# First weights' factors kept by units in DRAM, first keys in two halves, last block transposed on TensorE

## The chip, the cores and the metric

The kernel runs on one core of one Trainium2 chip. The metric is the device time of one execution in microseconds; a number is the median of several executions. A profile is one execution more, taken with the hardware profiler, and is a little longer than an unprofiled one. Engines are named as the profile does: PE is TensorE's matmul and PEld its weight load, DVE is VectorE, ACT is ScalarE, POOL is GpSimd, SP is SyncE, which only issues transfers here.

## The reference

Two blocks in a row. The first is attention with a hash: every query and key gets a bucket of 6 sign bits, and a query attends only to keys in its own bucket. The second is a layer with a squared ReLU. Cut to what matters:

```python
# q, k, v: (4, 8, 768, 64); proj: (64, 6); w_in: (512, 2048); w_out: (2048, 512)
q_bucket = bits(q @ proj > 0)                # 6 bits to one number
k_bucket = bits(k @ proj > 0)
scores = q @ k.T / 8
scores = where(q_bucket == k_bucket, scores, -1e9)
attn = softmax(scores)
x = (attn @ v) laid out as (3072, 512)       # tokens by heads
h = x @ w_in
g = maximum(h, 0) ** 2
out = g @ w_out                              # (3072, 512)
```

The weights arrive as 64-bit floats, and the kernel rounds them to 32 bits itself.

## The kernel before

Attention goes by 16 pairs of heads. For each pair PE hashes q and k with `projs`, ACT makes the bits, PE makes the scores (the bits' product keeps other buckets away), ACT takes the exponential, PE multiplies with v. Beside it DVE rounds the weights, piece by piece.

The layer is computed by a scheme of seven products in place of eight. Each matrix is cut in four blocks, and sums of blocks are the factors. For `w_in` these factors are made during attention and kept in DRAM as `w_in_7`, seven of them, and read back by units of 128 columns of the hidden layer, eight units for each of three chunks of 1024 tokens. For `w_out` the scheme is applied twice, with 49 factors in `w_out_49`, which are made beside the first chunk's hidden layer and written by POOL's queue.

```python
w_in_7 = p_d.tile([P, 7, NFT // 2, HF], FP32, name="w_in_7")     # 128, 7, 2, 1024, in DRAM

def keep_weight(i):
    ...                                      # once for each half of the columns
    for dst, f, h in (
        (w_in_7[:, 0], 0, 0), (w_in_7[:, 1], nf, 0), (w_in_7[:, 2], nf, 1), (w_in_21, 0, 1)
    ):
        nc.sync.dma_start(out=dst[:, :, at], in_=ins[j][:, f:f + nf, h])

def sums_in(c):                              # four times, 256 columns each
    ...
    for n in range(4):
        nc.sync.dma_start(out=w_in_7[:, 3 + n, :, c * NS:(c + 1) * NS], in_=sums[n])

def load_unit(n, pool=p_i):                  # two buffers, and one more at the start
    if n < NCHUNK * NR and n not in w_unit:
        r = n % NR
        w_unit[n] = pool.tile([P, 7, NFT // 2, P], FP32, name="w_unit", ...)
        nc.sync.dma_start(
            out=w_unit[n].rearrange("p l f c -> p (l f) c"),
            in_=w_in_7.rearrange("p l f c -> p (l f) c")[:, :, r * P:(r + 1) * P],
        )
```

The start. `load_first` brings q and k of the first pair, one head on SP's queue and one on ACT's; `keep_busy` gives PE matmuls on a constant so that it is not idle; `turn` hands out one of three PSUM buffers.

```python
def constants():
    nc.gpsimd.memset(projs, 0.0)
    for h in range(2):
        nc.gpsimd.dma_start(out=projs[h * D:(h + 1) * D, 0:N], in_=proj)
    ...

def first_keys():                            # the bits of the first pair's keys, on DVE
    bits[0, 1] = t = all_bits[0][1]
    for c in range(2):
        ...
        for h in range(2):
            nc.vector.tensor_scalar(out=t[...], in0=hashed[0, 1][at, h, 0:HS], ..., op0=ALU.is_gt)
        nc.vector.tensor_scalar(out=t[:, cut], in0=t[:, cut], scalar1=spans, scalar2=bases, ...)

load_first()
nc.vector.memset(busy, 1.0)
keep_busy(8)
...
first_features(0, 0)                         # PE transposes q, ACT copies
first_features(0, 1)
keep_busy(2, 256)
first_features(1, 0)                         # PE transposes k, DVE copies
hash_bits(0, turn("hash"), (0,))
first_features(1, 1)
banks = turn("hash")
for c in range(2):
    hash_bits(0, banks, (1,), (c,))
keep_busy(4)
signs(0, 0)                                  # ACT: the bits of q
first_keys()
for pr in range(NP):
    ...
    score(pr, 0)
    score(pr, 1)
    ...
```

The end. A block of the output is finished transposed: DVE turns it in squares of 32 into one of two buffers `ot`, and four transfers put the squares in their places.

```python
def put_out(i, ih, jh, n, o, lo=0):
    w = o.shape[1]
    ot = p_y.tile([P, HN], FP32, name="ot", bufs=2)[:, 0:w]
    nc.vector.transpose(out=ot, in_=o)
    ...
    for a in range(P // 32):
        queue = nc.gpsimd if (ih, jh) == (1, 1) else nc.sync
        if (i, ih, jh) == (NCHUNK - 1, 1, 0) and a % 2:
            queue = nc.scalar
        queue.dma_start(out=out[at, ...], in_=ot[a * 32:(a + 1) * 32]...)

def close(ih, jh, n):
    o = outs[ih, jh, n // 2]
    o[1] += 1
    if (i, ih, jh, n // 2) == (NCHUNK - 1, 1, 0, 1):      # the last block: by halves
        lo = n % 2 * QN
        put_out(i, ih, jh, n // 2, o[0][:, lo:lo + QN], lo)
    elif o[1] == 2:
        put_out(i, ih, jh, n // 2, o[0])
```

A second function, `general`, computes everything in the plain way when a guard finds inputs too large for the fast one. It does not run here, but it reads `w_in_7` too.

Of the kernel before, what the change touches and what calls it, by code (L numbers as in the profile page):

```python
# [8 lines left out]
FP32 = mybir.dt.float32  # L9
# [6 lines left out]
ALU = mybir.AluOpType  # L16
# [18 lines left out]
def kernel(  # L35
# [24 lines left out]
    PIECE = 512  # L60
# [19 lines left out]


    HF, HD, NR, NQ = DFF // 2, DM // 2, NFF // 2, NFF // 4
    w_in_7 = p_d.tile([P, 7, NFT // 2, HF], FP32, name="w_in_7")
    w_in_21 = p_d.tile([P, NFT // 2, HF], FP32, name="w_in_21")
    w_out_1 = p_d.tile([P, NFF, DM], FP32, name="w_out_1")
    w_out_49 = p_d.tile([7, P, 7, NQ, P], FP32, name="w_out_49")
# [15 lines left out]
    def turn(name):  # L102

        return ps_s.tile([P, 2, 512], FP32, name=name, tag="turn")
# [78 lines left out]
    def keep_weight(i):  # L183

        t = goals.pop(i)
        j, c = divmod(i, NIN)
        if j >= 2:
            nc.sync.dma_start(out=w_out_1[:, i - 2 * NIN], in_=t)
        elif c == NIN - 1:
            at = slice(j * PIECE, (j + 1) * PIECE)  # L190
            nf = NFT // 2
            for dst, f, h in (
                (w_in_7[:, 0], 0, 0), (w_in_7[:, 1], nf, 0), (w_in_7[:, 2], nf, 1), (w_in_21, 0, 1)
            ):
                nc.sync.dma_start(out=dst[:, :, at], in_=ins[j][:, f:f + nf, h])

# [21 lines left out]

    def constants():
        N = NBITS
        nc.gpsimd.memset(projs, 0.0)
        for h in range(2):
            nc.gpsimd.dma_start(out=projs[h * D:(h + 1) * D, 0:N], in_=proj)
        for t in (gains, lifts, spans, bases):
            nc.vector.memset(t, 0.0)
        nc.vector.memset(excess, -896.0)
        for h in range(2):
            r = h * D  # L230
            nc.vector.memset(gains[r:r + N + 1], -FAR / 2 * N)
# [28 lines left out]
    def load_first():  # L260

        for src, name in ((q, "q_nat"), (k, "k_nat")):
            t = p_qk.tile([P, SB, 2, D], FP32, name=name)
            for h, queue in enumerate((nc.sync, nc.scalar)):
                queue.dma_start(
                    out=t[:, :, h], in_=src[0, h].rearrange("(t p) d -> p t d", t=SB)
                )
            nat[0, name] = t

# [58 lines left out]
    def hash_bits(pr, banks, ws=(0, 1), cs=(0, 1)):  # L328


        for w in ws:
            hashed[pr, w] = banks
            for c in cs:
                g = 2 * w + c
                for h in range(2):
                    rows = slice(h * D, (h + 1) * D)
                    nc.tensor.matmul(  # L337
                        out=banks[g * NR_B:(g + 1) * NR_B, h, 0:HS], lhsT=projs[rows],
                        rhs=feat[pr, w][rows, c * HS:(c + 1) * HS], start=True, stop=True,
                    )  # L340

    def signs(pr, w):
        bits[pr, w] = t = all_bits[pr % 2][w]
        for c in range(2):
            at = slice((2 * w + c) * NR_B, (2 * w + c + 1) * NR_B)
            for h in range(2):
                nc.scalar.activation(  # L347
                    out=t[h * D:h * D + NR_B, c * HS:(c + 1) * HS], in_=hashed[pr, w][at, h, 0:HS],
                    func=ACTF.Sign, scale=HUGE, bias=lifts[at],
                )  # L350

    def first_keys():

        bits[0, 1] = t = all_bits[0][1]
        for c in range(2):
            at = slice((2 + c) * NR_B, (3 + c) * NR_B)
            cut = slice(c * HS, (c + 1) * HS)
            for h in range(2):
                nc.vector.tensor_scalar(
                    out=t[h * D:h * D + NR_B, cut], in0=hashed[0, 1][at, h, 0:HS],  # L360
                    scalar1=0.0, scalar2=None, op0=ALU.is_gt,
                )
            nc.vector.tensor_scalar(
                out=t[:, cut], in0=t[:, cut], scalar1=spans, scalar2=bases, op0=ALU.mult,
                op1=ALU.add,
            )

    def weigh(pr):

# [126 lines left out]
    def sums_in(c):  # L496

        j, h = divmod(c, 2)
        t, at = ins[j], slice(h * NS, (h + 1) * NS)
        nf = NFT // 2  # L500
        sums = [p_t.tile([P, nf, NS], FP32, name=f"s_in{n}", bufs=2) for n in range(4)]
        sums_a(
            t[:, 0:nf, 0, at], t[:, nf:NFT, 0, at], t[:, 0:nf, 1, at], t[:, nf:NFT, 1, at], *sums
        )
        for n in range(4):
            nc.sync.dma_start(out=w_in_7[:, 3 + n, :, c * NS:(c + 1) * NS], in_=sums[n])

# [17 lines left out]
    def load_unit(n, pool=p_i):  # L525

        if n < NCHUNK * NR and n not in w_unit:
            r = n % NR
            w_unit[n] = pool.tile([P, 7, NFT // 2, P], FP32, name="w_unit", bufs=2 if pool is p_i else 1)
            nc.sync.dma_start(  # L530
                out=w_unit[n].rearrange("p l f c -> p (l f) c"),
                in_=w_in_7.rearrange("p l f c -> p (l f) c")[:, :, r * P:(r + 1) * P],
            )

    def sums_x(i, n):

# [18 lines left out]
        spread(pr)  # L555

    with tc.manual_schedule():
        load_first()
        nc.vector.memset(busy, 1.0)
        keep_busy(8)  # L560
        make_identity(nc, ident)
        constants()
# [6 lines left out]
        keep_busy(2, 256)  # L569
        first_features(1, 0)  # L570
        hash_bits(0, turn("hash"), (0,))
        first_features(1, 1)
        banks = turn("hash")
        for c in range(2):
            hash_bits(0, banks, (1,), (c,))
        keep_busy(4)
        signs(0, 0)
        first_keys()

        for pr in range(NP):
# [243 lines left out]
            add_to(t, one, two)  # L826
            return t

        def put_out(i, ih, jh, n, o, lo=0):


            w = o.shape[1]
            ot = p_y.tile([P, HN], FP32, name="ot", bufs=2)[:, 0:w]
            nc.vector.transpose(out=ot, in_=o)  # L834
            m0 = ih * HD + n * P
            at = slice(i * NCH + jh * HN + lo, i * NCH + jh * HN + lo + w)
            for a in range(P // 32):
                queue = nc.gpsimd if (ih, jh) == (1, 1) else nc.sync
                if (i, ih, jh) == (NCHUNK - 1, 1, 0) and a % 2:
                    queue = nc.scalar  # L840
                queue.dma_start(
                    out=out[at, m0 + a * 32:m0 + (a + 1) * 32].rearrange("(c i) j -> i c j", i=32),
                    in_=ot[a * 32:(a + 1) * 32].rearrange("i (c j) -> i c j", j=32),
                )

        def project(i):

# [182 lines left out]
def general(tc, slow, ident, w_in_7, w_in_21, w_out_1, q, k, v, proj, out_v):  # L1030
# [19 lines left out]
    with ExitStack() as stack:  # L1050
# [4 lines left out]
        with tc.If(flag > 0), ExitStack() as inner:  # L1055
# [4 lines left out]
            for src, f, c in (  # L1060
                (w_in_7[:, 0], 0, 0), (w_in_7[:, 1], nf, 0), (w_in_7[:, 2], nf, hf), (w_in_21, 0, hf)
            ):
                nc.sync.dma_start(out=w_in[:, f:f + nf, c:c + hf], in_=src)
# [161 lines left out]
```

## Time and profile before

The median of three executions is 899.83 us (899.75 to 900.01). The profiled execution took 905.62 us, of which the span of the instructions is 903.8 us.

| stage of the span | us | what fills it |
|---|---|---|
| start, up to the first scores | 0 to 12.1 | loads, transposes, hash of the first pair |
| attention, 16 pairs | 12.1 to 337.7 | PE |
| first chunk's hidden layer | 337.7 to 441 | PE, with many transfers beside it |
| the rest of the layer | 441 to 892.6 | PE |
| end | 892.6 to 903.8 | last sums, transposes and transfers |

| transfer | number | KB each | median us to landing |
|---|---|---|---|
| `w_unit` from `w_in_7` (SP) | 24 | 896 | 5.5 |
| `w_in_7` from `in` (SP), `w_in_21` with it | 8 | 512 | 4.0 |
| `w_in_7` from the sums (SP) | 16 | 256 | 2.9 |
| `w_out_49` from sums and factors (POOL) | 28 | 448 | 7.0 and 7.3 |
| weights as they arrive (SP) | 32 | 512 | 5.4 and 4.1 |

How to read the profile's lines: in a timeline a line has its start, its length, the engine, the line of the kernel, the operation, the tile written and the tile read, sizes, the number of instructions merged into it, and in brackets how long the engine was idle just before and what ended that. A line of the stage table has the stretch, its length, each engine's busy time with its number of instructions, the clock granted to PE (1.00 is full), the busy share of the 16 DMA engines (rough, it can pass 1), and GB/s.

### The profile page before, as it was taken

The page shows a single profiled execution, that of the slowest core. Times are in us where ns is not written, and L with a number is a line of the kernel's source. Part 1 is how long each engine was busy: PE and PEld are TensorE (multiplying, and loading weights), DVE is VectorE, ACT ScalarE, POOL GpSimd, SP SyncE. Part 2 cuts the span into 40 slices and gives each one's busy share as a digit, 9 for nine tenths or more (in the row PEclk, how much of TensorE's full clock was granted, in tenths as well). Part 3 has the DMA queues.
Part 4 walks back from the last instruction along what each step waited for, and adds up shares of the span by engine and source line. Part 5 has one row for each costly group of instructions (what it writes and reads, how often), then busy time and mean ns, then how long its engine had stood idle before and what let it go on. Part 6 is the DMA issues. An engine that isn't in the chain of part 4 may idle for free.

```text
span 903.8 us, 11749 instructions
## 1 busy us (share of the span) xinstructions
PE 880.1 (97%) x4292; PEld 503.7 (56%) x4292; DVE 711.4 (79%) x991; ACT 376.0 (42%) x608; POOL 91.7 (10%) x149
## 2 busy tenths in 40 slices
PE   8999999999999999998999999999999999999995
PEld 4444444444444444443688854445888544458884
DVE  5899999999999977796777775668778666777874
ACT  5988788888888842221211112222111122221110
POOL 2000000000000002542000111112000111100002
PEclk9999999999999999998999999999999999999998
DMA  9578679899966318998765734557757455545475
GB/s 185 112 154 135 198 191 183 186 267 243 235 142 164 117 65 259 289 266 250 244 201 154 192 66 133 151 152 237 264 162 171 74 152 151 146 134 156 148 186 85
DMA packets 253407, 158.14 MB, mean 175 GB/s; under 512 B 166496, under 2 KB 215648, under 8 KB 253344
## 3 DMA queue, kind: packets, MB, share of 16 engines
q1 hardware_dynamic: 218448, 84.04, 40.3%
q10 hardware_dynamic: 24160, 37.89, 14.3%
q0 software_dynamic: 10736, 35.40, 12.7%
q8 instruction: 36, 0.59, 0.3%
q14 instruction: 27, 0.22, 0.1%
HBM read 119.28 MB, written 38.01 MB: 174 GB/s over the span
## 4 chain that ended last, share of the span: by engine, by line
PE 88%; DMA 5%; DVE 4%; ACT 1%; issue 1%; ACTq 0%; SPq 0%; DVEq 0%
PE acc L679 54%; PE st L385 17%; PE xo L414 14%; DMA w_unit<-w_in 3%; PE tot L433 2%; PE hash L337 2%; DMA out_dram<-ot 1%; DVE total L404 1%; DMA k_nat<-in_k_dram 1%; ACT bits L347 1%; DVE peaks L720 0%; DVE ot L834 0%; DVE b L769 0%; ACTq L809 0%; ACT e L389 0%
## 5 line engine op out<-in xcount | busy, mean ns | idle before, releaser
L679 PE MATMUL acc<-x,w_unit 128*128 128x512 f32 x384 | 172.2, 600 | 4.2 <-DMA w_unit<-w_in 4.2
L389 ACT ACTIVATE e<-st 128x1024 f32<-128x1024 f32 x192 | 145.2, 810 | 50.1 <-PE st L385 45.6
L385 PE MATMUL st<-feat,feat 64*128 64x512 f32 (+1 forms) x768 | 150.4, 483 | 0.0
L414 PE MATMUL xo<-e,v_nat 128*64 128x512 f32 (+1 forms) x768 | 134.8, 492 | 0.0
L679 PE MATMUL acc<-b,leaf 128*128 128x256 f32 x600 | 132.9, 379 | 0.0
L679 PE MATMUL acc<-t_x,w_unit 128*128 128x512 f32 x288 | 127.8, 593 | 0.5 <-ACT one L686 0.5
L679 PEld LDWEIGHTS acc<-x,w_unit 128*128 128x128 f32 x384 | 73.8, 193 | 96.8 <-issue 90.6
L679 PEld LDWEIGHTS acc<-b,leaf 128*128 128x128 f32 x600 | 114.0, 190 | 16.8 <-issue 1.4
L404 DVE TENSOR_TENSOR total<-total,e 128x1536 f32<-128x1536 f32 x58 | 101.9, 1757 | 3.8
L414 PEld LDWEIGHTS xo<-e,v_nat 128*64 128x64 f32 x768 | 51.3, 136 | 82.4 <-issue 75.0
L679 PEld LDWEIGHTS acc<-t_x,w_unit 128*128 128x128 f32 x288 | 54.5, 190 | 70.2 <-issue 67.7
L768 DVE TENSOR_TENSOR h<-acc,two 128x512 f32<-128x512 f32 x24 | 16.6, 691 | 89.8 <-PE acc L679 89.8
L385 PEld LDWEIGHTS st<-feat,feat 64*128 64x128 f32 x768 | 66.1, 188 | 33.9 <-issue 25.2
L679 PE MATMUL acc<-t,leaf 128*128 128x256 f32 x336 | 76.6, 380 | 0.7 <-ACT one L686 0.4
L686 ACT COPY two<-acc 128x512 f32<-128x512 f32 (+1 forms) x45 | 21.9, 486 | 132.6 <-PE acc L679 120.3
L347 ACT ACTIVATE bits<-hash,lifts 32x384 bf16<-32x384 f32 x124 | 71.0, 573 | 4.9 <-PE hash L337 1.6
L686 ACT COPY one<-acc 128x512 f32<-128x512 f32 (+1 forms) x45 | 21.9, 486 | 122.4 <-PE acc L679 76.7
L679 PEld LDWEIGHTS acc<-t,leaf 128*128 128x128 f32 x336 | 63.6, 190 | 10.5 <-DVE t L492 1.1
L769 DVE SCALAR_TENSOR_TENSOR b<-h 128x512 f32<-128x512 f32 x96 | 64.3, 690 | 2.5
L385 PE MATMUL st<-bits,bits 64*128 64x256 bf16 (+1 forms) x384 | 63.2, 325 | 2.4 <-ACT e L389 1.2
L679 PE MATMUL acc<-b_t,leaf 128*128 128x256 f32 x240 | 54.2, 380 | 2.0 <-issue 2.0
L679 PEld LDWEIGHTS acc<-b_t,leaf 128*128 128x128 f32 x240 | 45.4, 190 | 8.8 <-issue 2.7
(124 smaller groups left out, 867.1 us busy)
## 6 DMA issues: line engine op xcount, KB each, us to landing
leaf<-w_out ACTq DMA_DIRECT2D x142, 256.0 KB, 3.0
w_unit<-w_in SPq DMA_DIRECT2D x24, 896.0 KB, 5.5
raw<-in_moe_w_in_dram SPq DMA_DIRECT2D x16, 512.0 KB, 5.4
raw<-in_moe_w_out_dram SPq DMA_DIRECT2D x16, 512.0 KB, 4.1
w_out<-sums POOLq DMA_DIRECT2D x16, 448.0 KB, 7.0
v_nat<-in_v_dram SPq DMA_DIRECT2D x16, 384.0 KB, 4.3
x_all<-x_t SPq DMA_DIRECT2D x16, 384.0 KB, 3.1
x<-x_all POOLq DMA_DIRECT2D x3, 2048.0 KB, 12.0
```

The lines of the kernel that those rows point to most:

```text
L337: nc.tensor.matmul(out=banks[g * NR_B:(g + 1) * NR_B, h, 0:HS], lhsT=projs[rows], rhs=feat[pr, w][rows, c * HS:(c + 1) * HS], start=True, ...
L347: nc.scalar.activation(out=t[h * D:h * D + NR_B, c * HS:(c + 1) * HS], in_=hashed[pr, w][at, h, 0:HS], func=ACTF.Sign, scale=HUGE, bias=li ...
L385: nc.tensor.matmul(out=st[:, h, 0:hi - lo], lhsT=src[pr, 1][rows, key], rhs=src[pr, 0][rows, lo:hi], start=first, stop=not first,)
L389: nc.scalar.activation(out=e[:, :, lo:hi], in_=st[:, :, 0:hi - lo], func=ACTF.Exp, scale=scale)
L404: nc.vector.tensor_tensor(out=totals[pr], in0=totals[pr], in1=weights[pr, kt][:, :, 0:S], op=ALU.add)
L414: nc.tensor.matmul(out=xo[h * D:(h + 1) * D, lo:hi], lhsT=nat[pr, "v_nat"][:, h, kt * D:(kt + 1) * D], rhs=weights[pr, kt][:, h, lo:hi], s ...
L433: nc.tensor.matmul(out=tot[g * 32:(g + 1) * 32, 0:HS], lhsT=ones, rhs=src[:, h, c * HS:(c + 1) * HS], start=src is srcs[0], stop=src is sr ...
L679: nc.tensor.matmul(out=acc[to], lhsT=a(i), rhs=b(i), start=first and i == 0, stop=last and i == n - 1, skip_group_check=True,)
L686: nc.scalar.copy(out=t, in_=acc[of])
L768: nc.vector.tensor_tensor(out=h, in0=one, in1=two, op=ALU.add)
L769: nc.vector.scalar_tensor_tensor(out=out[:, r], in0=h, scalar=0.0, in1=h, op0=ALU.max, op1=ALU.mult)
```

## The change

Three parts. First, the factors in DRAM are laid out by unit, so that what `load_unit` reads is one stretch per partition; the writes are cut accordingly, and `general` reads them in the new order. Second, the bits of the first pair's keys are made in two halves, the second after the first scores; with it the projection comes by one transfer on ACT's queue in place of two on POOL's, and the memsets of `busy` and `projs` go first on DVE. Third, the last output block is transposed on PE, copied by ACT and DVE, and written by one transfer for each half; half of the transfers of the block before it move from ACT's queue to POOL's.

```diff
-    w_in_7 = p_d.tile([P, 7, NFT // 2, HF], FP32, name="w_in_7")
+    w_in_7 = p_d.tile([NR, P, 7, NFT // 2, P], FP32, name="w_in_7")
 ...
-            for dst, f, h in (
-                (w_in_7[:, 0], 0, 0), (w_in_7[:, 1], nf, 0), (w_in_7[:, 2], nf, 1), (w_in_21, 0, 1)
-            ):
-                nc.sync.dma_start(out=dst[:, :, at], in_=ins[j][:, f:f + nf, h])
+            for n, f, h in (0, 0, 0), (1, nf, 0), (2, nf, 1):
+                put_factor(n, j * PIECE, ins[j][:, f:f + nf, h])
+            nc.sync.dma_start(
+                out=w_in_21[:, :, j * PIECE:(j + 1) * PIECE], in_=ins[j][:, 0:nf, 1]
+            )
+
+    def put_factor(n, c, t):
+        for f in range(NFT // 2):
+            rs = t[:, f].rearrange("p (r c) -> p r c", c=P)
+            nc.sync.dma_start(
+                out=w_in_7[c // P:c // P + rs.shape[1], :, n, f].rearrange("r p c -> p r c"), in_=rs
+            )
 ...
         for n in range(4):
-            nc.sync.dma_start(out=w_in_7[:, 3 + n, :, c * NS:(c + 1) * NS], in_=sums[n])
+            put_factor(3 + n, c * NS, sums[n])
 ...
-            nc.sync.dma_start(
-                out=w_unit[n].rearrange("p l f c -> p (l f) c"),
-                in_=w_in_7.rearrange("p l f c -> p (l f) c")[:, :, r * P:(r + 1) * P],
-            )
+            nc.sync.dma_start(out=w_unit[n], in_=w_in_7[r])
```

```diff
     def constants():
-        nc.gpsimd.memset(projs, 0.0)
-        for h in range(2):
-            nc.gpsimd.dma_start(out=projs[h * D:(h + 1) * D, 0:N], in_=proj)
 ...
     def load_first():                        # in its loop over q and k
+            if src is q:
+                nc.scalar.dma_start(
+                    out=projs[:, 0:NBITS],
+                    in_=proj.rearrange("(o d) n -> o d n", o=1).to_broadcast([2, D, NBITS]),
+                )
 ...
-    def first_keys():
+    def first_keys(c, banks):                # hash, compare and scale one half
+        hash_bits(0, banks, (1,), (c,))
 ...
+        nc.vector.memset(busy, 1.0)
+        nc.vector.memset(projs, 0.0)
         load_first()
-        nc.vector.memset(busy, 1.0)
 ...
         hash_bits(0, turn("hash"), (0,))
+        signs(0, 0)
+        first_keys(0, turn("hash"))
         first_features(1, 1)
-        banks = turn("hash")
-        for c in range(2):
-            hash_bits(0, banks, (1,), (c,))
         keep_busy(4)
-        signs(0, 0)
-        first_keys()
 ...
             score(pr, 0)
+            if pr == 0:
+                first_keys(1, turn("hash"))
             score(pr, 1)
```

```diff
                 if (i, ih, jh) == (NCHUNK - 1, 1, 0) and a % 2:
-                    queue = nc.scalar
+                    queue = nc.gpsimd
 ...
+        def put_last(n, o):
+            row, col = n // 2, n % 2
+            tp = ps_m.tile([P, 512], FP32, name=f"acc{col}")[:, 0:QN]
+            for t in range(QN // P):
+                nc.tensor.transpose(
+                    out=tp[:, t * P:(t + 1) * P], in_=o[:, t * P:(t + 1) * P], identity=ident
+                )
+            ot = p_y.tile([P, HN], FP32, name="ot", bufs=2)[:, 0:QN]
+            if col:
+                nc.scalar.copy(out=ot, in_=tp)
+            else:
+                nc.vector.tensor_copy(out=ot, in_=tp)
+            (nc.sync if col else nc.scalar).dma_start(out=out[...], in_=ot...)
 ...
                 if (i, ih, jh, n // 2) == (NCHUNK - 1, 1, 0, 1):
-                    lo = n % 2 * QN
-                    put_out(i, ih, jh, n // 2, o[0][:, lo:lo + QN], lo)
+                    if o[1] == 2:
+                        for col in (1, 0):
+                            put_last(n - n % 2 + col, o[0][:, col * QN:(col + 1) * QN])
```

More of the change, by code (lines that the diff above doesn't have):

```diff
@@ L189, in keep_weight @@
         elif c == NIN - 1:
-            at = slice(j * PIECE, (j + 1) * PIECE)
             nf = NFT // 2
-            for dst, f, h in (
-                (w_in_7[:, 0], 0, 0), (w_in_7[:, 1], nf, 0), (w_in_7[:, 2], nf, 1), (w_in_21, 0, 1)
-            ):
-                nc.sync.dma_start(out=dst[:, :, at], in_=ins[j][:, f:f + nf, h])
+            for n, f, h in (0, 0, 0), (1, nf, 0), (2, nf, 1):
[9 more added lines that the diff above has]
+            )
     HUGE, SMALL, NR_B = 2.0**64, 2.0**-70, 32
@@ L350, in signs @@
                 )
-    def first_keys():
-        bits[0, 1] = t = all_bits[0][1]
-        for c in range(2):
[L356 to L361, printed above, removed]
-                )
+    def first_keys(c, banks):
+        if c == 0:
+            bits[0, 1] = all_bits[0][1]
+        t = bits[0, 1]
+        hash_bits(0, banks, (1,), (c,))
+        at = slice((2 + c) * NR_B, (3 + c) * NR_B)
+        cut = slice(c * HS, (c + 1) * HS)
+        for h in range(2):
             nc.vector.tensor_scalar(
-                out=t[:, cut], in0=t[:, cut], scalar1=spans, scalar2=bases, op0=ALU.mult,
-                op1=ALU.add,
-            )
+                out=t[h * D:h * D + NR_B, cut], in0=banks[at, h, 0:HS],
+                scalar1=0.0, scalar2=None, op0=ALU.is_gt,
+            )
+        nc.vector.tensor_scalar(
+            out=t[:, cut], in0=t[:, cut], scalar1=spans, scalar2=bases, op0=ALU.mult,
+            op1=ALU.add,
+        )
     def weigh(pr):
@@ L529, in load_unit @@
             w_unit[n] = pool.tile([P, 7, NFT // 2, P], FP32, name="w_unit", bufs=2 if pool is p_i else 1)
-            nc.sync.dma_start(
-                out=w_unit[n].rearrange("p l f c -> p (l f) c"),
-                in_=w_in_7.rearrange("p l f c -> p (l f) c")[:, :, r * P:(r + 1) * P],
-            )
+            nc.sync.dma_start(out=w_unit[n], in_=w_in_7[r])
     def sums_x(i, n):
@@ L571 @@
         hash_bits(0, turn("hash"), (0,))
+        signs(0, 0)
+        first_keys(0, turn("hash"))
         first_features(1, 1)
-        banks = turn("hash")
-        for c in range(2):
-            hash_bits(0, banks, (1,), (c,))
         keep_busy(4)
-        signs(0, 0)
-        first_keys()
         for pr in range(NP):
@@ L827, in whole, with put_out @@
             return t
-        def put_out(i, ih, jh, n, o, lo=0):
-            w = o.shape[1]
-            ot = p_y.tile([P, HN], FP32, name="ot", bufs=2)[:, 0:w]
+        def put_out(i, ih, jh, n, o):
+            ot = p_y.tile([P, HN], FP32, name="ot", bufs=2)
             nc.vector.transpose(out=ot, in_=o)
             m0 = ih * HD + n * P
-            at = slice(i * NCH + jh * HN + lo, i * NCH + jh * HN + lo + w)
+            at = slice(i * NCH + jh * HN, i * NCH + (jh + 1) * HN)
             for a in range(P // 32):
@@ L844, in put_out @@
                 )
+        def put_last(n, o):
[4 more added lines that the diff above has]
+                    out=tp[:, t * P:(t + 1) * P], in_=o[:, t * P:(t + 1) * P], identity=ident
+                )
+            ot = p_y.tile([P, HN], FP32, name="ot", bufs=2)[:, 0:QN]
[3 more added lines that the diff above has]
+                nc.vector.tensor_copy(out=ot, in_=tp)
+            lo = (NCHUNK - 1) * NCH + col * QN
+            (nc.sync if col else nc.scalar).dma_start(
+                out=out[lo:lo + QN, HD + row * P:HD + (row + 1) * P].rearrange(
+                    "(t p) j -> p t j", p=P
+                ),
+                in_=ot.rearrange("p (t j) -> p t j", j=P),
+            )
         def project(i):
@@ L1059, in general @@
             nf, hf = NFT // 2, NFF // 2 * P
[L1060 to L1063, printed above, removed]
+            for n, f, c in (0, 0, 0), (1, nf, 0), (2, nf, hf):
+                for i in range(nf):
+                    nc.sync.dma_start(
+                        out=w_in[:, f + i, c:c + hf].rearrange("p (r c) -> p r c", c=P),
+                        in_=w_in_7[:, :, n, i].rearrange("r p c -> p r c"),
+                    )
+            nc.sync.dma_start(out=w_in[:, 0:nf, hf:2 * hf], in_=w_in_21)
             nc.sync.dma_start(out=w_out, in_=w_out_1)
```

## The prediction

> **What bounds the kernel now.** I read four views in this order: the head of the page (which engine fills the span), the stage table (where that engine is not full), the timeline of each stage with a hole, and the groups of the tiles that the hole names.
>
> The head of the page: span, busy time, granted TensorE clock by slice.
>
> ```profile
> span 903.8 us, 11749 instructions
> PE 880.1 (97%) x4292; PEld 503.7 (56%) x4292; DVE 711.4 (79%) x991; ACT 376.0 (42%) x608; POOL 91.7 (10%) x149
> ...
> PEclk9999999999999999998999999999999999999998
> ```
>
> TensorE (PE) is busy 880.1 of 903.8 us, so everything that is not matmul is worth 23.7 us at most, plus what a lowered clock costs. One slice in the middle shows 8 instead of 9. A change of layout and of edges can only win in those holes.
>
> The stage table: start and end of the stretch, its length, busy time of PE, PE's weight load, DVE, ACT, POOL, then granted clock, DMA share, GB/s.
>
> ```profile
> 31.70:317.80 286.10, 286.10 (x2148) 131.31 (x2151) 267.36 (x326) 241.52 (x354) 0.79 (x1) 1.00 0.76 178
> 337.70:425.00 87.30, 83.07 (x187) 36.47 (x188) 68.22 (x96) 19.34 (x33) 35.65 (x40) 0.96 0.95 275
> 878.50:903.80 25.30, 14.05 (x67) 11.92 (x65) 12.77 (x28) 1.49 (x4) 5.21 (x8) 0.87 0.55 105
> ```
>
> The attention stage (31.7 to 317.8) has no hole: whatever is changed in it is free as long as PE stays full. The first chunk's hidden layer (337.7 to 425) lacks 4.2 us, at a clock of 0.96 and with the DMA engines 95% busy. The tail lacks 11.3 us. The first 31.7 us lack 4.6 us.
>
> The timeline around the middle hole (start, length, engine, line, operation, tiles, count, idle before and what ended it):
>
> ```profile
> 394.65 3.94 POOL L974 DMA_DIRECT2D w_out<-sums  x4
> ...
> 403.71 2.96 POOL L974 DMA_DIRECT2D w_out<-factors  x3 [5.11 <-DVE factors L489]
> ...
> 414.22 6.36 PE L679 MATMUL acc<-x,w_unit 128*128 128x512 f32 x8 [4.23 <-DMA w_unit<-w_in]
> ```
>
> The load of unit 6 is issued at 398.00, when unit 4's buffer is freed, and lands at 414.2: 16.2 us, though the page's median for this load is 5.5. PE stands 4.23 us. Then its first 8 matmuls take 6.36 us; the same 8 matmuls take 3.70 us at 337.62. The hole costs 4.23 + 2.66 = 6.9 us.
>
> The head and the tail, from the timeline:
>
> ```profile
> 6.88 0.32 PEld L300 LDWEIGHTS tp<-ident,k_nat 128*128 128x128 f32 x3 [0.58 <-DMA k_nat<-in_k_dram]
> 8.46 2.35 ACT L347 ACTIVATE bits<-hash,lifts 32x384 bf16<-32x384 f32 x4 [1.59 <-PE hash L337]
> 10.44 1.12 DVE L359 TENSOR_SCALAR bits<-hash 32x384 bf16<-32x384 f32 x2 [1.02 <-PE hash L337]
> ...
> 895.00 0.45 DVE L834 STREAM_TRANSPOSE ot<-o 128x256 f32<-128x256 f32 x1 [1.58 <-DMA out_dram<-ot]
> 896.44 0.45 DVE L834 STREAM_TRANSPOSE ot<-o 128x256 f32<-128x256 f32 x1 [0.69 <-DMA out_dram<-ot]
> ```
>
> The first keys land at 6.88, the four signs of q are ready at 10.81, and the first scores begin at 12.08, after the keys' own bits. In the tail the last two output transposes wait for a free `ot` buffer, not for PE, which is done at 892.6.
>
> [...] 28 writes of `w_out` of 448 KB in runs of 512 B would be 25,088 packets if each run were one, but the whole software queue counts 10,736. So those writes travel in large packets, while the 24 loads of `w_unit` (1,792 runs of 512 B each, 43,008 in all) sit in a hardware queue of 218,448 packets with a mean of 385 B. [...] 592 ns is the median of these matmuls and 1,222 ns the longest.
>
> **The change, part by part.**
>
> *Factors by units.* The load of a unit becomes 128 runs of 7,168 B instead of 1,792 of 512 B[...]. At 398 about 7 writes have been issued since 391.66, 196 KB per engine; at 300 GB/s (18.75 KB per us and engine, what the stage's 275 to 322 GB/s show) they last until 402.1, so some 77 KB per engine are left. [...] (77 + 56) / 18.75 = 7.1 us[...]. It lands near 406; PE needs it at 410.0. Before, [...] (77 + 56 + 84) / 18.75 = 11.6 us, plus 2.5 us for the small runs (5.5 alone against 3), near 412 (measured 414.2). So the wait and the slow matmuls go: 6.9 us. I count 6.4, because without a profile the stall may be shorter; the profiled run took 905.62 us against 899.83.
>
> *What the layout costs.* The factors are now written by unit and by row half: 6 writes become 12 and 16 become 32, in runs of 512 B. They lie under the full attention stage. SyncE issued 4 of them in 5.27 us at 91.78; 7 make about 9.2, so the next raw weights come 4 us later. Their load was issued at 97.10, lands some 5.4 us later, and DVE uses it at 107.95: about 5 us of slack. I put 0.2 us on this.
>
> *First keys in two halves.* PE hashes the first half of the keys before it transposes the second, and the first scores need only the first half. DVE then has one pair of comparisons (1.12) and one scaling (0.38) ahead of them instead of two. With keys landing at the same time, the first scores would start when the signs of q are done, 10.85 instead of 12.08: 1.2 us won, and ACT, which leads this stage, moves with them. The second half's hash and comparisons go behind the first scores and are not needed before the fourth key tile.
>
> *The projection's load.* It moves from POOL to ACT's queue, between q and k of the second head, behind a memset on DVE. Its source begins with a broadcast dimension of 2[...]. A hardware packet takes 40.3% x 16 x 903.8 us / 218,448 = 27 ns; [...] I take 2.4 us for the keys' delay. Then the signs end at 13.2 and scores start 1.1 us late instead of 1.2 early. [...] the keys lose about 0.5 us and the start wins 0.7. I lean two to one on the first: (2 x 1.1 - 0.7) / 3 = +0.5 us.
>
> *The last block.* DVE's sums end at about 893.8, PE transposes four 128x128 squares, ACT and DVE copy. Both copies still take `ot` buffers: ACT's is free at 894.9, DVE's only when the block before has landed. That block now goes half over POOL, issued 0.65 us apiece to 894.0 and landing 2.8 later, so about 896.6. Copy 0.4, one DMA instead of two: issued at 897.0 and landed 3.0 later at 900.0. Before, the last issue was at 897.8 and landed 3.1 later at 900.9. I take -0.7 us.
>
> Sum: -6.4 + 0.2 + 0.5 - 0.7 = -6.4 us; 899.83 becomes 893.4.
>
> **Rivals.** (a) The load stays late: the DMA engines are 95% to 102% busy there, and [...] the unit lands after 410 as before. For it: the total bytes are unchanged. Against it: the same load alone takes 5.5 us. Time: near 899.5. (b) The wait moves: once PE is 6.9 us ahead, unit 7 (issued at 410, needed at 422) or the first leaves (needed at 434, their source written until about 425) become late. DVE is 22% idle here (68.22 of 87.30). Time: 896 to 898. (c) The keys are not delayed and everything comes in: -6.9 - 0.7 - 0.7, so 891.5. (d) The raw weights come too late and DVE, 93% busy in attention, pushes PE: 1 us for each of six pairs at the worst, 899.
>
> **Range and chances.** Centre 893.4. Full success gives 891.5, a little less with a better tail 890.5; a half stall plus a late start gives 897.5. Two per cent is 18 us, three quarters of all 23.7 us of holes, so faster by over 2% needs a cause that I don't see (0.02). Slower by 2% needs PE starved through attention (0.02).
>
> **What would show it.** Middle: no PE wait on `w_unit` near 410, landing under 12 us, no matmul of 1,222 ns, eight units in 96 us. Start: the keys' first transpose near 9.3 and scores near 13.2 [...]. Attention: PE full, and DVE waits on `raw` under 1 us. Tail: DVE's last copy waits for `out_dram`. I am wrong if the middle still waits, or a wait for `leaf` or unit 7 takes its place.

## The result, and the profile after

The changed kernel takes 899.55 us (median of 6 executions, 897.95 to 900.80). The kernel before takes 900.5 us in the six executions beside it (899.75 to 901.73). The ratio is 0.9988, with a 95% interval of 0.9974 to 1.0002: no difference that these runs can tell from none, where 893.4 us was predicted.

The head of the page of the changed kernel, as the prediction showed it for the kernel before:

```profile
span 898.2 us, 11774 instructions
PE 878.5 (98%) x4296; PEld 502.8 (56%) x4296; DVE 711.0 (79%) x991; ACT 376.6 (42%) x609; POOL 91.7 (10%) x148
PEclk9999999999999999999999999999999999999998
```

The span is 898.2 us against 903.8, the slice with clock 8 in the middle is gone, and PE has 19.7 us of holes instead of 23.7. By the profiles alone the change wins 5.6 us. By the times it wins about one, which the interval does not tell from none. The two profiles are of executions that stand differently to their kernels' medians: the one before took 905.62 us where its median was 899.83, the one after took 899.94 where its median is 899.55. This turned out to be the main point of the case. That a profile is by itself a little longer, as was said at the start, does not explain it and does not hold here: in the twelve runs below the profiled execution lies between 2.1 us under (e10) and 0.9 us over (e8) its kernel's median.

The stage table of the changed kernel, for the three stretches shown of before (columns as there; the third is again the last 25 us of the span):

```profile
31.70:317.80 286.10, 285.42 (x2134) 130.54 (x2132) 266.62 (x325) 240.76 (x353) 0.91 (x1) 1.00 0.77 179
337.70:425.00 87.30, 87.30 (x218) 38.86 (x215) 70.92 (x102) 20.31 (x35) 35.61 (x40) 1.00 0.86 266
873.00:898.20 25.20, 13.93 (x65) 11.24 (x63) 11.71 (x26) 1.86 (x5) 6.50 (x10) 0.87 0.48 90
```

The first chunk's hidden layer is now full: PE 87.30 of 87.30 us at clock 1.00, with the DMA engines 86% busy instead of 95%. The attention stage, full before, has a hole of 0.7 us. The tail lacks 11.3 us, as before.

The middle in the changed kernel's timeline: the load of unit 6, and the matmuls that waited for it before.

```profile
400.57 0.32 SPq L542 DMA_DIRECT2D w_unit<-w_in  x1
...
408.96 3.60 PE L688 MATMUL acc<-x,w_unit 128*128 128x512 f32 x8
```

The line of the matmuls has no bracket, so PE did not wait, and eight of them take 3.60 us. Over all 24 loads the landing took 4.4 / 4.7 / 10.8 us (least, median, most); before it was 5.2 / 5.5 / 19.2.

The start in the changed kernel's timeline:

```profile
1.50 1.14 ACTq L274 DMA_DIRECT2D projs<-in_proj_dram  x1
...
2.67 0.39 ACTq L270 DMA_DIRECT2D k_nat<-in_k_dram  x1
...
8.47 0.52 PE L310 MATMUL tp<-ident,k_nat 128*128 128x128 f32 x3 [1.69 <-DMA k_nat<-in_k_dram]
...
12.28 0.39 PE L397 MATMUL st<-bits,bits 64*128 64x512 bf16 x2 [0.47 <-ACT bits L357]
...
13.56 1.51 ACT L401 ACTIVATE e<-st 128x1024 f32<-128x1024 f32 x2 [1.32 <-PE st L397]
14.00 0.83 PE L347 MATMUL hash<-feat,projs 64*32 64x384 f32 x4
...
16.07 4.75 ACT L401 ACTIVATE e<-st 128x1024 f32<-128x1024 f32 x6 [0.99 <-PE st L397]
```

ACT begins to issue the projection's load at 1.50, after the memset of `projs`, and takes 1.14 us for it, so the keys' load behind it goes out at 2.67 instead of 1.28, and the keys are transposed at 8.47 instead of 6.88. The first scores start at 12.28, 0.2 us later than before, because only half of the keys is prepared ahead of them. But the other half's hash now stands on PE between the first scores and the second, for 0.83 us, and ACT, which leads this stage, is idle for 0.99 us after its first two exponentials. In the kernel before all eight run as one row:

```profile
13.37 6.37 ACT L389 ACTIVATE e<-st 128x1024 f32<-128x1024 f32 x8 [2.55 <-PE st L385]
```

The first pair's total comes at 37.08 us; before it came at 35.99.

The tail in the changed kernel's timeline:

```profile
886.40 0.71 DVE L842 STREAM_TRANSPOSE ot<-o 128x512 f32<-128x512 f32 x1
...
887.40 1.29 POOL L849 DMA_DIRECT2D out_dram<-ot  x2 [1.41 <-DVE ot L842]
...
887.93 0.77 PE L859 MATMUL acc<-ident,o 128*128 128x128 f32 x4 [1.09 <-DVE o L828]
888.40 0.37 ACT L864 COPY ot<-acc 128x256 f32<-128x256 f32 x1 [5.47 <-PE acc L859]
888.80 0.39 SPq L868 DMA_DIRECT2D out_dram<-ot  x1
892.92 0.42 DVE L866 COPY ot<-acc 128x256 f32<-128x256 f32 x1 [4.72 <-DMA out_dram<-ot]
893.38 0.40 ACTq L868 DMA_DIRECT2D out_dram<-ot  x1
```

PE has transposed the last block at 888.7, but DVE's copy of the second half starts at 892.92. It waits 4.72 us for an `ot` buffer. The chain of waits of the same kernel says which transfer still holds it:

```profile
887.45 0.59 DVE o L828 x2
888.04 4.80 DMA out_dram<-ot
892.85 0.03 DVEq L866
```

It is the second of POOL's two transfers of the block before, issued at 888.04 and landed 4.80 us later. The last transfer is issued 6.5 us after the last product's end (886.84); before it was about 5.2 us (897.8 and 892.55).

### The profile page after: what moved, and what is told of

Same layout as the page of the kernel before. It is cut to its first block, busy times and chain, and to the rows that moved or that the text cites. A ratio compares the mean times of both kernels' runs of the same rounds, so it can differ in the third digit from the quotient of the medians.

```text
span 898.2 us, 11774 instructions
## 1 busy us (share of the span) xinstructions
PE 878.5 (98%) x4296; PEld 502.8 (56%) x4296; DVE 711.0 (79%) x991; ACT 376.6 (42%) x609; POOL 91.7 (10%) x148
## 4 chain that ended last, share of the span: by engine, by line
PE 90%; DVE 4%; DMA 3%; ACT 1%; issue 1%; SPq 0%; DVEq 0%; ACTq 0%
PE acc L688 58%; PE st L397 16%; PE xo L426 13%; PE tot L445 2%; PE hash L347 2%; DMA out_dram<-ot 1%; DVE total L416 1%; DMA raw<-in_moe_w_out_dram 1%; ACT bits L357 1%; DMA k_nat<-in_k_dram 1%; DVE peaks L729 0%; DVE b L778 0%; DVE ot L842 0%; DVE h L777 0%; DVE b_t L504 0%
## 5 line engine op out<-in xcount | busy, mean ns | idle before, releaser
L688 PE MATMUL acc<-x,w_unit 128*128 128x512 f32 x384 | 169.3, 592 | 0.0
## 6 DMA issues: line engine op xcount, KB each, us to landing
x<-x_all POOLq DMA_DIRECT2D x3, 2048.0 KB, 12.1
```

Source lines behind the costliest of these rows:

```text
L688: nc.tensor.matmul(out=acc[to], lhsT=a(i), rhs=b(i), start=first and i == 0, stop=last and i == n - 1, skip_group_check=True,)
```

## The experiments

Two theories were set against each other. In the first, called theory 2 in the expectations, the prediction's mid term is right and something else in the change gives most of it back. In the rival, called theory 1 there, the hole of 6.9 us was a feature of one long execution, and there was never so much to win. Theory 3 came later: the changed kernel's raw weights come late. So did theory 4: the new tail costs more beside the layout. The first four runs take the change apart; the later ones test what was found. Times are medians; each ratio is to the kernel before, run on the same chip beside it, with its 95% interval.

| run | what it is | us | before, us | ratio (interval) |
|---|---|---|---|---|
| e1_before | the kernel before, nothing changed | 900.47 | 900.24 | 1.0002 (0.9993 to 1.0010) |
| e2_units | the layout alone | 896.36 | 900.24 | 0.9958 (0.9944 to 0.9971) |
| e3_keys | the first keys alone | 901.21 | 900.24 | 1.0010 (1.0003 to 1.0017) |
| e4_tail | the last block alone | 900.17 | 900.24 | 1.0002 (0.9993 to 1.0010) |
| e5_after | the whole change, again | 899.64 | 900.65 | 0.9990 (0.9981 to 0.9999) |
| e6_after_raw | the whole change, raw weights asked for first | 899.05 | 900.65 | 0.9978 (0.9969 to 0.9986) |
| e7_best | layout, raw first, start of before, mended tail | 893.91 | 900.65 | 0.9922 (0.9908 to 0.9935) |
| e8_keys_projs_last | the first keys alone, projection behind the keys | 899.99 | 900.65 | 0.9989 (0.9979 to 1.0000) |
| e9_units_again | the layout alone, again | 896.92 | 901.35 | 0.9954 (0.9940 to 0.9969) |
| e10_units_keys | layout and first keys | 899.39 | 901.35 | 0.9973 (0.9963 to 0.9984) |
| e11_units_tail | layout and last block | 898.96 | 901.35 | 0.9973 (0.9963 to 0.9984) |
| e12_tail_tmp | mended tail alone | 898.91 | 901.35 | 0.9974 (0.9965 to 0.9983) |

**The kernel before, profiled afresh.** Edit: none.

> The kernel before, unchanged, in a fresh profile. Theory 1 (the wait for unit 6 in the profile shown was an accident of that one execution, which took 905.62 us against 899.83): span near 898, wait of PE for w_unit near 410 under 1 us, first chunk's 8 units in 96 to 98 us. Theory 2 (the wait is in every execution, and the change gives its gain back elsewhere): span near 903, wait about 4 us, 8 units in 103 us. Time equal to before under both.

The profiled execution took 900.78 us, close to the median. Its timeline at the hole (SyncE's line merges two issues, at 398.38 and 410.40, so its length is not that of a load):

```profile
398.38 12.53 SPq L530 DMA_DIRECT2D w_unit<-w_in  x2
...
411.77 3.70 PE L679 MATMUL acc<-x,w_unit 128*128 128x512 f32 x8 [1.40 <-DMA w_unit<-w_in]
```

The load of unit 6 is late here too: 13.3 us to its landing at 411.73. But PE waits 1.40 us and not 4.23, and the eight matmuls after it take 3.70 us and not 6.36. The hole is 1.5 us instead of 6.9. PE's granted clock in the 6.36 us of the first profile was 0.58, and the longest of the matmuls on `w_unit` took 1,222 ns; here the clock is 1.00 from 398 to 412, and none of them takes over 697 ns. The eight units of the first chunk take 97.91 us here and took 103.39 in the first profile: that difference of 5.5 us covers all that lies between the two profiled executions (905.62 and 900.78, 4.8 us). Four other profiles without the layout (e3, e4, e8, e12) show this wait at 1.5, 1.4, 0.9 and 1.5 us. Of the 133 timed executions of the kernel before, here and beside the other runs, two took 905 us or more; what they spent it on no profile shows. The rival theory holds, with a wait that is longer than the 1 us it allowed: the hole of 6.9 us belongs to a rare execution.

The chain of waits of the same run shows that the late loads hurt in a second place (start, length, what):

```profile
411.77 24.32 PE acc L679 x56
436.10 15.03 DMA w_unit<-w_in
...
451.15 0.33 ACTq L809
...
451.57 0.38 ACT one L686
...
451.99 67.61 PE acc L679 x312
```

A later load takes 15.0 us to land. By the chain ACT's next work, a leaf load and then the copy `one`, waits for it, and PE then waits 0.39 us for the copy. The prediction had looked at one hole and not at what another slow load did to ACT's order.

**The layout alone.** The edit is the first diff of the change, at its core:

```diff
-                in_=w_in_7.rearrange("p l f c -> p (l f) c")[:, :, r * P:(r + 1) * P],
+            nc.sync.dma_start(out=w_unit[n], in_=w_in_7[r])
```

> Only the factors' layout by units. Theory 1: nothing to win in the middle; the later raw weights cost up to 1.5 us, so 0 to +1.5 us against before. Theory 2: -5 to -6 us. In both the wait for raw of 1.5 us near pair 9 should be there, and no wait for w_unit.

0.9958, so 3.8 us faster: neither theory had this, theory 1 too little and theory 2 too much. The wait for the raw weights, expected under both, did not occur. The same stretch of its chain of waits:

```profile
394.99 121.93 PE acc L684 x475
516.92 0.39 issue
517.32 96.73 PE acc L684 x228
```

From 395 to 614 nothing but PE stands in the chain, apart from 0.39 us of issue: both waits of e1 are gone. Eight units take 96.24 us. The loads land in 4.4 / 4.6 / 10.5 us, against 5.2 / 5.4 / 19.0 in e1.

**The first keys alone.** The edit is the second diff; its two ends:

```diff
+            if src is q:
+                nc.scalar.dma_start(out=projs[:, 0:NBITS], in_=proj...to_broadcast([2, D, NBITS]))
...
+            if pr == 0:
+                first_keys(1, turn("hash"))
```

> Only the first keys in two halves, with the projection on ACT's queue. Both theories: +1.1 us against before, the shift that the profile of the changed kernel shows from the second pair on (24.69 against 23.61).

1.0010, so 0.9 us slower, and the interval leaves 1 out. The first scores start at 12.17 and the first pair's total comes at 36.95 (e1: 12.47 and 36.38). The start itself is not late; the loss comes between the first scores and the first total, as in the profile of the whole change.

**The last block alone.** The edit is the third diff; its core:

```diff
-                    queue = nc.scalar
+                    queue = nc.gpsimd
...
+            ot = p_y.tile([P, HN], FP32, name="ot", bufs=2)[:, 0:QN]
```

> Only the last block. Both theories: from the last matmul to the end of the span the changed kernel takes 11.4 us and before 11.3, so 0 +- 0.5 us; DVE's last copy waits 4 to 5 us for out_dram. If my prediction of the tail holds after all: -0.7 us.

1.0002: nothing. The span ends 11.31 us after the last product matmul, in e1 11.09. The prediction's -0.7 us did not come. DVE's last copy waits 4.88 us for an `ot` buffer, as in the whole change.

**The whole change again, and with the raw weights first.** e5 has no edit. e6 asks for the second raw weights of each pair ahead of the factors' writes:

```diff
+            if pr > 0:
+                load_weight(b)
+            for put in puts:
+                put()
+            puts.clear()
...
-                load_weight(b)
...
-            put_factor(3 + n, c * NS, sums[n])
+            puts.append(lambda n=n: put_factor(3 + n, c * NS, sums[n]))
```

> The changed kernel once more, on the chip of the next three. The parts alone gave -3.9 (layout), +0.9 (keys), 0 (tail). If parts only add up: -3.0 us against before. If the keys' shift makes the raw weights late (theory 3, the wait of 1.5 us for raw near 211 us in its profile): -1 to -1.5 us, and the wait is in the profile again.

> The changed kernel, with the second weights of each pair asked for before anything else on SyncE's queue, and the factors' writes behind that. Theory 3: no wait of DVE for raw, 1.5 to 2 us faster than the changed kernel, -3 us against before. If the raw weights are not what makes the parts not add up: same as the changed kernel.

e5 gives 0.9990, in line with the first result and with theory 3, but the wait that theory 3 named is not in its profile. e6 gives 0.9978, about 1 us better than e5 and not the 1.5 to 2 expected; the intervals touch, so the gain is likely and not certain, and that it comes from the raw weights is not shown. The wait itself is seen in the first profile of the changed kernel, in its timeline of the ninth pair:

```profile
193.01 5.82 SPq L201 DMA_DIRECT2D w_in<-s_in  x8
...
204.50 0.43 SPq L128 DMA_DIRECT2D raw<-in_moe_w_out_dram  x1
...
212.12 0.43 DVE L141 TENSOR_SCALAR power<-raw 128x512 uint32<-128x512 uint32 x1 [1.53 <-DMA raw<-in_moe_w_out_dram]
...
218.12 1.62 PE L347 MATMUL hash<-feat,projs 64*32 64x384 f32 x16 [0.68 <-DVE feat L334]
```

SyncE spends 5.8 us on eight writes of factors, asks for the raw weights at 204.50, and DVE stands 1.53 us for them. PE, full until there, then stands 0.68 us for DVE's transposes and takes 1.62 us for a hash that took 0.88 us one pair earlier: the step from the ninth pair's total to the tenth's takes 22.05 us instead of 20.55. No other profile has this; the step is 20.55 to 20.62 us in all of them, e5 and e6 included. Nor do the eight writes alone bring it: e5 spends 5.88 us on them and asks for the raw weights at 204.59, as late, and its DVE goes on at 210.62. So the cost was seen in one execution, and why the load came late there stays open.

**The projection behind the keys.** Edit on the first keys alone: the same load, after the loop over q and k.

```diff
-            if src is q:
-                nc.scalar.dma_start(out=projs[:, 0:NBITS], ...)
         ...
+        nc.scalar.dma_start(out=projs[:, 0:NBITS], ...)
```

> Only the first keys in two halves, but the projection's load on ACT's queue behind the keys' load, not ahead of it. The keys are then issued at 1.28 as before and not at 2.67. If the delay of the keys is the issue time alone: first scores near 11.0, and with 0.9 us for the second half's hash between the first scores -0.3 us against before. If the second half's hash between the scores is all of the cost: +0.9 us as with the projection ahead.

The keys' load is back at 1.29, their transposes at 6.97, and the first scores start at 11.22, 0.9 us before those of the kernel before, though the hash first waits 0.87 us for the projection. The ratio is 0.9989, about 1 us faster than before (0.3 was expected) with an interval that touches 1, and about 1.9 us better than e3. The issue order is thus what delayed the keys. The timeline shows what remains:

```profile
13.08 1.51 ACT L392 ACTIVATE e<-st 128x1024 f32<-128x1024 f32 x2 [1.32 <-PE st L388]
13.52 0.84 PE L338 MATMUL hash<-feat,projs 64*32 64x384 f32 x4
...
15.59 4.75 ACT L392 ACTIVATE e<-st 128x1024 f32<-128x1024 f32 x6 [0.99 <-PE st L388]
```

The hole of 0.99 us on ACT is there to the hundredth, whenever the first scores start: it is the price of the second half's hash between the scores. The first pair's total comes at 36.57 (e1: 36.38), so the start that was won is spent there.

**The parts in pairs.** e9 is the layout alone, e10 adds the first keys, e11 adds the last block; the edits are the diffs above.

> Only the layout by units, a second time, on the chip of the next three. It gave -3.9 us (interval -5.0 to -2.6): the same again if it holds; the stages between 434 and 702 should be 0.5 to 1 us shorter each than before, as in its first profile.

> Layout and keys together, tail as before. The changed kernel gave -1.0 us where the parts add up to -3.0. If keys are what costs more beside the layout (theory 3, later raw weights): -1 us. If they only add: -3.0 us.

> Layout and last block together, start as before. If the new tail costs more beside the layout (theory 4: the layout alone ended 9.8 us after the last matmul, all kernels with the new tail 11.4 us after it): -2.3 us. If they only add: -3.9 us.

The layout alone gives 0.9954, so 4.1 us. Each of the other two parts takes back 0.0019 of the ratio, 1.7 us, though the last block cost nothing without the layout; the intervals just overlap (up to 0.9969 and from 0.9963). The sum -4.1 + 1.7 + 1.7 = -0.7 us matches what the whole change shows (0.9988 and 0.9990, so -1.1 and -0.9); worked out from the medians of the table it is about 0. e11 is where theory 4 had it; e10, with -2.4 us, lies between its two expectations, and why the keys cost 0.9 us alone and 1.7 us here is not shown. The milestones of the profiles, in us:

| | e1 before | e2 layout | e9 layout | e10 layout, keys | e11 layout, tail | after | e12 mended tail | e7 |
|---|---|---|---|---|---|---|---|---|
| first pair's total | 36.38 | 36.02 | 36.10 | 36.95 | 36.21 | 37.08 | 36.30 | 36.14 |
| first hidden matmul | 338.00 | 337.64 | 337.73 | 338.58 | 337.90 | 340.19 | 337.93 | 337.77 |
| first leaf matmul | 435.91 | 433.88 | 433.96 | 434.82 | 434.13 | 436.43 | 435.90 | 434.00 |
| last product ends | 887.91 | 883.34 | 885.20 | 885.03 | 885.23 | 886.84 | 887.79 | 883.68 |
| from there to the end | 11.09 | 9.76 | 10.70 | 10.57 | 12.07 | 11.36 | 8.91 | 7.92 |
| of this, until the last store has landed | 8.0 | 7.8 | 8.7 | 8.3 | 9.9 | 9.2 | 6.6 | 5.9 |
| of this, after it | 3.1 | 2.0 | 2.0 | 2.3 | 2.2 | 2.1 | 2.3 | 2.1 |

From the first hidden matmul to the last product the profiles without the layout (e1, e3, e4, e8, e12) take 548.2 to 549.9 us, mean 549.3; the eight with it 545.7 to 547.5, mean 546.5. So the layout wins 2.8 us there. The rest of its 4.1 us lies at the end: with the old tail the span ends 9.76 to 10.70 us after the last product where the layout is in (e2, e9, e10), 11.09 to 11.75 where it is not (first profile of before, e1, e3, e8). The new tail takes 11.3 to 12.1 us in either case. That is why the last block costs nothing alone and 1.7 us beside the layout.

The last two rows of the table say where the old tail loses its 1 us. Its last store lands 7.8 to 8.7 us after the last product with the layout and 7.9 to 8.3 us without it, so the layout does not speed up the stores; the new tail's lands 9.2 to 9.9 us after it in both cases, about 1 us later. What differs is the time behind the last landing: 3.1 to 3.5 us in the four profiles with the old tail and the old layout, 2.0 to 2.3 us in all others. In the first profile of the kernel before, SyncE's first step after the branch of the guard comes 2.7 us behind the branch (898.89 to 901.61), 1.2 us after the last store has landed (900.42), and e1 has the same wait of 2.7 us; in e2, e9 and e10 the wait is 1.2 to 1.8 us. The new tail lands so late that such a delay does not show: in the changed kernel the step comes 3.2 us behind the branch, at 893.03, and the last store lands only at 896.02. So about 1 us of the layout's gain has nothing to do with its loads. What makes SyncE ready sooner is not shown; the layout also changes the code of `general` that this branch skips.

**A tail without the wait.** Two words are changed in the last block: the copies go to `tmp` buffers, which nothing holds at that time, and the block before goes over ACT's queue again. e12 has this alone; e7 has it with the layout, the raw weights first, and the start of the kernel before.

```diff
-                    queue = nc.gpsimd
+                    queue = nc.scalar
...
-            ot = p_y.tile([P, HN], FP32, name="ot", bufs=2)[:, 0:QN]
+            ot = p_y.tile([P, QN], FP32, name="tmp", bufs=2)
```

> Only the last block on TensorE, but its copies go to the buffers of the small sums, and the block before it goes by ACT's queue as it did. If the wait for an output buffer is what makes the new tail worth nothing: DVE's last copy runs 5 to 6 us sooner and the end comes 2.5 to 3.5 us sooner than before. If the transfers set the end anyway: -0.5 us.

> Layout by units with the weights asked for first, the start of before, and the last block on TensorE with its copies in the buffers of the small sums, so that they wait for no transfer; the block before it goes by SyncE's and ACT's queues. -3.9 us for the layout; DVE's last copy then runs near PE's end + 1.5 us instead of + 6, and the end comes when the block before has landed, 2.5 to 3 us sooner: -6.5 us against before, 893.7. If the end is set by the last transfers' own landing: -5 us.

e12 gives 0.9974, so 2.3 us faster, just short of what was expected, where the change's own tail gave nothing. Its timeline, at the end:

```profile
888.88 0.77 PE L850 MATMUL acc<-ident,o 128*128 128x128 f32 x4 [1.09 <-DVE o L819]
889.35 0.37 ACT L855 COPY tmp<-acc 128x256 f32<-128x256 f32 x1 [5.21 <-PE acc L850]
889.68 0.42 DVE L857 COPY tmp<-acc 128x256 f32<-128x256 f32 x1 [0.53 <-PE acc L850]
...
890.14 0.40 ACTq L859 DMA_DIRECT2D out_dram<-tmp  x1
```

DVE's copy waits 0.53 us, for PE and not for a buffer. The last transfer is issued 2.4 us after the last product's end (887.79), in the changed kernel 6.5 us. e7 gives 893.91 us, 0.9922 (0.9908 to 0.9935): 7.0 us faster than the kernel before, and faster than the changed kernel by more than both intervals. Its parts alone give -4.1 - 2.3 = -6.4.

## Why the prediction was wrong, step by step

**The mid term was mis-sized, and this is the first step that failed.** The prediction put it so: "So the wait and the slow matmuls go: 6.9 us. I count 6.4, because without a profile the stall may be shorter; the profiled run took 905.62 us against 899.83." The warning was in the sentence, and was priced at half a microsecond. The measured hole is 1.5 us in e1 (1.40 of wait, 0.1 of slower matmuls), and of the excess of 5.8 us in the profiled execution the first chunk's units make 5.5. The prediction's own sum, an estimate from bytes and rate, said so: it has the old load landing near 412, with PE in need of it at 410.0, and e1 has 411.73; the measured 414.2 was taken in its stead. Any hole whose size is close to such an excess has to be taken as part of it.

**What it said the middle would show came.** No PE wait on `w_unit` near 409, no slow matmuls, the late load landing under 12 us (9.7 in e2, 8 estimated), eight units in 96.24 us: each came as written. The sums behind the 8 us and the 412 were the author's estimates: no trace shows in what order the engines took the loads and the writes. Rival (a), a load that stays late, is out, and so is (b): 96.24 us, and a chain in e2 that is all PE from 395 to 516, leave no room for a wait that takes the place of the old one.

**The layout's gain past the hole was not predicted.** It wins 2.8 us from the first hidden matmul to the last product, of which the first chunk's units give 1.7 (97.91 to 96.24) and the later stages the rest, and about 1 us behind the last landing. The chain of e1 names one of these places, ACT's work behind a load of 15 us. That the layout still won 4 us, where 6.2 were predicted for it, is in good part luck.

**The layout's cost was put at 0.2 us.** It is 1.5 us in one profile of the changed kernel and 0 in the other, as in e2, e9 and e10. The raw weights were not asked for 4 us later: at the place of the wait e5 asks at 204.59 and e1 at 203.23, of which the later start makes 0.8 us. Rival (d) named the wait that came, 1.53 us, but it came once and not by the delay of the issue alone.

**The start's +0.5 came out near the truth by luck.** Alone it costs 0.9 us, by another way. The sum weighed 1.1 us late twice against 0.7 us won once, from a delay of the keys of 2.4 or 0.5 us; both delays were the author's estimates, shown by no trace. The keys' delay is 1.6 us (8.47 against 6.88), but not because the projection's transfer crawls: the keys' load on ACT's queue landed 5.66 us after its issue, and 5.56 us after it in the kernel before. What delays them is the 1.14 us that ACT spends to issue that load, and 0.2 us that it waits for the memset before it. The larger error was to see only the moment of the first scores. They start only 0.2 us later, since less work stands ahead of them; ACT's hole of 0.99 us after the second exponential was not in the sum at all.

**The tail's -0.7 was the second step that failed: it is zero alone, and +1.7 us beside the layout.** That DVE's last copy waits for `out_dram` was predicted. Its length was not: the transfer it waits for landed 4.80 us after its issue on POOL's queue, where 2.8 was taken. (The old tail's last store landed at 900.4, half a microsecond before the 900.9 of the prediction's sum.) So the last store landed about 1 us later than the old tail's. e12 takes the wait away with another buffer and another queue, and lands it 6.6 us after the last product; which of the two does it was not taken apart, but DVE's copy then waits for PE alone.

**The sum, corrected.** By the ratios of the pairs the prediction was 2.1 us off on the layout (-6.2 against -4.1), 1.2 on the keys (+0.5 against +1.7) and 2.4 on the tail (-0.7 against +1.7). By the profiles: middle and later stages -2.8, start +1.1 (37.08 against 35.99), raw weights between 0 and +1.5, tail 11.4 against 11.1 to 11.8, so about 0: an estimate of -1.7 to -0.2 us, where -1.1 and -0.9 were measured.

## What to carry to other kernels

Before a hole in a profile is priced, hold the profiled execution's time against the median of the timed ones; if it is longer by about the size of the hole, profile again, for the hole may be the excess itself. A part that frees one thing (a transpose, a first result) is worth what the next resource allows: here the output buffer and the engine that leads the stage took the gain back, and another buffer and queue made the difference between 0 and 2.3 us. Measure the parts of a change beside each other and not only alone: one part cost nothing alone and 1.7 us in company, because without the layout the end had a delay that its later stores hid.

## What the runs showed of the hardware

- A PE wait can cost more than its length. In the first profile of the kernel before PE stood 4.23 us; its granted clock fell to 0.50 after 2.8 us of that and stayed there for 6.8 us, and the next eight matmuls took 6.36 us. After waits of 0.9 to 1.5 us (e1, e3, e4, e8, e12) no matmul on `w_unit` took over 697 ns, against a median of 592 and the 1,222 ns of that profile. The length alone did not decide: at the end of the kernel before the clock fell 4.9 us after PE's last work (892.55 to 897.47), at the end of the changed kernel 2.8 us after it (888.70 to 891.47).
- The same 896 KB, loaded as 128 runs of 7,168 B instead of 1,792 of 512 B, landed in 4.6 to 4.8 instead of 5.4 to 6.4 us at the median, and in 10.4 to 10.8 instead of 19.0 to 19.3 us at the worst. The worst load of the two kernels lay in the first chunk, where the busy share of the DMA engines was 0.95 before and 0.86 after. The three latest loads of the kernel before (19.2, 16.2 and 15.1 us) took 10.8, 9.7 and 4.6 us in the changed kernel.
- A load of 3 KB with a broadcast source kept ACT for 1.14 us to issue in the changed kernel and for 1.15 us in e8, where the loads of q and k beside it took 0.39 to 0.67 us. On the way to the first result this issue time, and not the transfer, was most of the cost: the keys' load behind it landed 5.66 us after its own issue, and 5.56 us in the kernel before. That the broadcast is the reason was not tested.
